# A chunked state scan feeding a gated two-layer product: the second scan moved ahead in the prologue, and the early loads gathered in one queue

## The chip, the cores and the metric

The kernel runs on one core of one Trainium2 chip. The metric is the device time of one execution in microseconds (us); lower is better. Five engines work side by side, each through its own list of instructions in order: TensorE (PE, matrix products), VectorE (DVE), ScalarE (ACT), GpSimd (POOL) and SyncE (SP, which here only issues loads and stores). An engine waits where an instruction needs something that another engine or a load has not finished yet. Loads and stores are moved by 16 DMA engines, and wait in the queue of the engine that issues them: SP's queue (with a few of ACT's) and POOL's.

## The reference

The first half is a state-space scan (Mamba-2's form) on x (4 batches, 8 heads, 768 steps, 32 wide), a decay a per head and step, and B and C (16 wide). Cut to what matters, per chunk:

```python
la = log(clip(a, 1e-6, 1)); cum = cumsum(la)
M = (C @ B.T) * exp(cum_i - cum_j) * causal       # inside a chunk
y = M @ x + (C @ state) * exp(cum)                # and from the chunks before
state = exp(sum(la)) * state + sum_j(B_j x_j * exp(cum_last - cum_j))
```

The result, 3072 tokens of 256 numbers, goes through two layers with float32 weights w_in (256 x 2048) and w_out (2048 x 256), which are given in double precision:

```python
h = x @ w_in
g = h * (1 / (1 + exp(-h)))                       # SiLU
out = g @ w_out
```

## The kernel before, in words

**Units and pairs.** The tokens are cut into 12 *units* of 256 (three to a batch). A unit's scan gives XF[u], its 256 tokens as input of the two layers. Units are taken in pairs: pair 0 is units 0 and 1. For pair 0 the two layers run in plain float32 products: f_s1(u, j) multiplies XF[u] with weight block j (j = 0 to 7, 256 columns of w_in) on PE and takes the SiLU on ACT; f_s2(j), "m" in the lists below, multiplies with weight block 8 + j of w_out. From pair 1 on, the products are split into three parts at a faster format (s1_h, s1_d, s2, s2_d), driven by step(s); that part of the kernel is not changed. There are two PSUM banks ("hp", function half) for the results of first products, so a product needs the bank whose SiLU, two products earlier, is done.

**A unit's scan.** Its steps are: f_TP or f_T (transposes of B and C, on PE or DVE, with copies on ACT), f_T2 (CE = C by head parity, ACT), f_Ek or f_E1 (E, the decay matrix, as a running scan on DVE), f_B (B times the last decay), f_P0 and f_P (clipping the decay, on POOL, and its running product pfx on DVE), f_C (C times pfx), f_G (C B^T, small products on PE into a bank "gy"), f_D0 (B^T x, the same bank), f_M (E times f_G's result, DVE, two halves), f_S (the state from chunk to chunk, DVE), f_SM (ACT), f_Y (all of it together on PE) and f_X (copy to XF on ACT). f_M and f_S need f_D0, and f_Y needs f_M, f_SM and f_C. E needs ab[u], the decay spread over partitions. For units 0 and 1 PE makes ab from ach (f_Ab); for unit 2 it is loaded back from a_first, a small copy of the first decays that f_A writes to DRAM; from unit 3 on from a_zero, which f_A3 writes together with a_in, the source of pz. So f_P of unit 3 and f_E1 of unit 3 need a round trip: load acl, clip it on POOL (f_A2), store a_in and a_zero (f_A3), and load pz (load_pa) and ab (load_ab) back.

**Weights.** A block n (0 to 15) is loaded in double precision (load_w, 512 KB, tile raw). ACT makes two parts of it (w_size: wu, wv), DVE three operations on them (w_bits), POOL the last addition, which gives the float32 block w32[n]. raw, and later the split inputs xh, xl, xd of a pair, share a ring of six buffers, so raw of block 6 takes the buffer of block 0, and so on: a load waits until its buffer's last reader is done.

**The order.** Nothing is scheduled automatically: each engine runs its instructions in the order in which this Python program names them. Lines 698 to 783 are the prologue: scan of unit 0, block 0 and so on, with the scan of unit 1 in between, written out by hand. Then `steps` (L844) names first products (u, j) with texts that say what is put behind each: "b5" is w_bits(5), "s6" w_size(6), "r10" the load of block 10, "2:T1" for unit 2 the stages T and 1, where a stage's letters are those of `stage` (T transposes, P pfx, 1 and 2 the halves of the scan E, B, C, D = f_G and f_D0, S, s = f_SM, M, Y = f_Y and f_X, h, l, d the split of XF, a = load_ab of the next unit, L all loads of a unit). A second list does the same for m0 to m5. busy(n) puts dummy products on PE.

Of the kernel before, what the change touches and what calls it, by code (L numbers as in the profile page):

```python
# [33 lines left out]
def kernel(  # L34
# [22 lines left out]
    nc = tc.nc  # L57
# [58 lines left out]
    def load_n(u, i, q, ks=(0, 1)):  # L116
        b, t0 = at(u)
        if i == 1:
            if u not in tbc:
                tbc[u] = block("tbc0")[:, 0:256].rearrange("p (k h n) -> p k h n", k=2, h=H)  # L120
        elif u not in bn:
            bn[u] = (block("bn0")[:, 0:256].rearrange("p (k h n) -> p k h n", k=2, h=H) if u in (0, 1, 3) else
                     loads.tile([128, 2, H, N], FP32, name="bn"))
        for k in ks:
            q.dma_start(out=(bn, tbc)[i][u][:, k], in_=(B, C)[i][b, :, t0 + 128 * k:t0 + 128 * k + 128].rearrange("h p n -> p h n"))
# [12 lines left out]
    def load_x(u, q, ks=(0, 1)):  # L138
        b, t0 = at(u)
        if u not in xt:  # L140
            xt[u] = loads.tile([128, 2, H, D], FP32, name="xt", bufs=2)
        for k in ks:
            q.dma_start(out=xt[u][:, k], in_=x[b, :, t0 + 128 * k:t0 + 128 * k + 128].rearrange("h p d -> p h d"))
# [31 lines left out]
    def load_w(n, q):  # L175
        j = n % 8
        src = wi[:, :, j * WF:(j + 1) * WF] if n < 8 else wo[:, 2 * j:2 * j + 2]
        if src.dtype == FP32:
            w32[n] = block("w32")
            q.dma_start(out=two(w32[n]), in_=src)  # L180
            return
        t = raw[n] = quad.tile([128, 2, WF, 2], U32, name="raw", tag="quad")
        q.dma_start(out=t.rearrange("p k f two -> p k (f two)"), in_=src.bitcast(U32))

    def w_size(n, what="uv"):
        if n in raw:
            if "u" in what:
                u = wu[n] = block("wu")
                nc.scalar.activation(two(u), raw[n][:, :, :, 1].bitcast(FP32), AF.Abs)
            if "v" in what:  # L190
                v = wv[n] = block("wv")
                nc.scalar.activation(two(v), raw[n][:, :, :, 0], AF.Copy, scale=2.0 ** -51, bias=2.0)

    def w_bits(n, parts=1):
        if n in raw:
            u, v, hi = two(wu.pop(n)), two(wv.pop(n)).bitcast(U32), raw[n][:, :, :, 1]
            w32[n] = block("w32")
            for i in range(parts):
                fs = slice(WF // parts * i, WF // parts * (i + 1))
                if i == 0 or n == 0:  # L200
                    ws = fs if n == 0 else slice(0, WF)
                    ui = u[:, :, ws].bitcast(U32)
                    nc.vector.tensor_scalar(out=u[:, :, ws], in0=u[:, :, ws], scalar1=LEAST, scalar2=MOST,
                                            op0=ALU.max, op1=ALU.min)
                    nc.vector.tensor_scalar(out=ui, in0=ui, scalar1=3, scalar2=None, op0=ALU.logical_shift_left)
                    nc.vector.scalar_tensor_tensor(out=v[:, :, ws], in0=hi[:, :, ws], scalar=0x80000000, in1=v[:, :, ws],  # L206
                                                   op0=ALU.bitwise_and, op1=ALU.bitwise_or)
                nc.gpsimd.tensor_tensor(out=two(w32[n])[:, :, fs].bitcast(U32), in0=u[:, :, fs].bitcast(U32),  # L208
                                        in1=v[:, :, fs], op=ALU.add)
# [42 lines left out]
    for n in range(2):  # L252
        load_w(n, nc.sync)
    load_a(1)
    load_w(2, nc.sync)
    load_w(3, nc.sync)
    load_x(1, nc.sync, (0,))

    def f_A():
        nc.vector.tensor_scalar(out=ach[A0:A1], in0=ach[A0:A1], scalar1=1.0, scalar2=1e-6, op0=ALU.min, op1=ALU.max)  # L260
        nc.vector.memset(ach[A0:A1, :, 0:1], 0.0)
        nc.sync.dma_start(out=a_first, in_=ach[A0:A1])
# [3 lines left out]
    def f_A1():  # L266
        for b in range(1, batch):
            nc.sync.dma_start(out=acl[NC0 * (b - 1):NC0 * b],
                              in_=bass.AP(tensor=a.tensor, offset=a.offset + b * H * S, ap=[[Q, NC0], [S, H], [1, Q]]))
# [51 lines left out]
    nc.scalar.activation(misc[:, 2 * UT - 1:], idle[:, 0:1], AF.Silu)  # L321
    early(6)
    f_A()
    hm = const.tile([128, H], FP32, name="hm")
    nc.gpsimd.memset(hm, 1.0)
    nc.gpsimd.affine_select(out=hm, in_=hm, pattern=[[-N, H]], compare_op=ALU.is_ge,
# [42 lines left out]
    def f_Ek(u, k, hs=slice(0, H)):  # L369
        scan_E(u, H * k + hs.start, hs.stop - hs.start, ab.pop((u, k, hs.start))[:, hs])  # L370
# [77 lines left out]
    def f_M(u, k):  # L448
        m = E[u].rearrange("p k (g e) t -> p k g (e t)", e=2)
        nc.vector.tensor_tensor(out=m[:, k], in0=DP[u][:, :, 128 * k:128 * k + 128], in1=m[:, k], op=ALU.mult)  # L450
# [78 lines left out]
    def f_s1(u, j):  # L529
        hp = two(half("hp"))  # L530
        for i in range(2):
            for kc in range(KC):
                nc.tensor.matmul(out=hp[:, i], lhsT=two(w32[j])[:, kc, 128 * i:128 * i + 128],  # L533
                                 rhs=two(XF[u])[:, kc], start=(kc == 0), stop=(kc == KC - 1))
        GT[u, j] = block("gT")
        nc.scalar.activation(two(GT[u, j]), hp, AF.Silu)
        if j == 7:
            XF.pop(u)
# [168 lines left out]
    for e in range(2):  # L707
        f_T2(0, e)
    nc.scalar.activation(BH[0], new_dp(0)[:, 2, 256:512], AF.Copy)
    load_w(4, nc.sync)  # L710
    load_ab(2, nc.sync)
    load_a(2)
    f_A1()
    f_Ek(0, 0, slice(4, 8))
    f_Ek(0, 1, slice(0, 4))
    busy(1, 10, acc("zero"))
# [7 lines left out]
    f_M(0, 0)  # L724
    w_size(0, "u")
    f_C(0, nc.gpsimd)
    load_x(1, nc.gpsimd, (1,))
    load_n(1, 1, nc.gpsimd)
    f_S(0)
    f_SM(0)  # L730
# [5 lines left out]
    f_Y(0)  # L736
    busy(2)
    f_X(0)
    load_n(2, 1, nc.gpsimd, (0,))
    f_Ek(1, 0)  # L740
    w_bits(1, 2)
    load_n(2, 1, nc.gpsimd, (1,))
    w_size(2)
    f_s1(0, 0)
    w_size(3)
    f_Ek(1, 1)
    w_bits(2, 2)
    f_s1(0, 1)
    f_TP(1)
    for e in range(2):  # L750
        f_T2(1, e)
    load_bcx(3, "c")
    for n in range(5, 8):
        load_w(n, nc.sync)
    f_B(1, nc.gpsimd)
    f_P0(1, nc.gpsimd)
    w_bits(3, 2)
    w_size(4)
    f_s1(0, 2)
    f_G(1)  # L760
    f_D0(1)
    w_bits(4, 2)
    f_P(1)
    f_C(1, nc.gpsimd)
    f_P0(2, nc.gpsimd)
    load_n(2, 0, nc.gpsimd)
    load_x(2, nc.gpsimd)
    f_A2(True)
    f_A2(False)
    f_A3()  # L770
    for n in range(8, 10):
        load_w(n, nc.sync)
    load_pa(3, nc.sync)
    f_S(1)
    f_SM(1)
    f_M(1, 0)
    f_M(1, 1)
    f_P(2)
    f_s1(0, 3)
    f_s1(0, 4)  # L780
    f_Y(1)
    f_X(1)
    w_size(5)

    def stage(u, what):
        for c in what:
            if c == "L":
                load_unit(u)
            elif c == "a":
                load_ab(u + 1, nc.sync)  # L790
            elif c == "n":
                load_n(u, 0, nc.gpsimd)
            elif c == "x":
                load_x(u, nc.gpsimd)
            elif c == "T":
                if 0 < u < UPB:
                    f_TP(u)
                else:
                    f_T(u, 0)
                    f_T(u, 1)  # L800
                f_T2(u, 0)
                f_T2(u, 1)
            elif c == "P":
                f_P(u)
            elif c in "12":
                f_E1(u, int(c) - 1, 2)
            elif c == "B":
                f_B(u)
            elif c == "C":
                f_C(u)  # L810
            elif c == "D":
                f_G(u)
                f_D0(u)
            elif c == "M":
                f_M(u, 0)
                f_M(u, 1)
            elif c == "S":
                f_S(u)
            elif c == "s":
                f_SM(u)  # L820
            elif c == "Y":
                f_Y(u)
                f_X(u)
            elif c == "h":
                f_xh(u)
            elif c == "l":
                f_xl(u)
            elif c == "d":
                f_xd(u)
# [4 lines left out]
    def todo(text):  # L834

        for step in text.split():
            if ":" in step:
# [3 lines left out]
            n = int(step[1:].split(".")[0])  # L841
            {"b": w_bits, "s": w_size, "h": w_h, "l": w_l, "d": w_d, "v": partial(w_d, vector=True), "m": f_s2, "p": s1_d, "r": load_r}[step[0]](n)

    steps = ((1, 0, "2:T1 b5 s6"), (1, 1, "2:C2Ba r10"), (1, 2, "3:nx b6 r11 s7"), (1, 3, "2:DSsM r12"),  # L844
             (1, 4, "b7 r13 s8"), (0, 5, "3:T s9"), (1, 5, "2:Y b8 r14"), (0, 6, "3:1PC s10"),
             (1, 6, "b9 r15 3:2B s11 h0 l0"), (0, 7, "2:h s12"), (1, 7, "3:D b10 3:SsM"))
    for u, j, text in steps:
        f_s1(u, j)
        todo(text)
    for text in ("m0 b11 s13 2:l h1 l1", "m1 3:Y b12 s14 2:d d0 4:L 3:h h2 l2", "m2 b13 s15 3:l d1 h3 l3",  # L850
                 "m3 b14 3:d d2 h8 l8 v3", "m4 b15 p0 d8 h4 l4 v4 h5 l5", "m5 4:T v5 h9 l9 v9"):
        todo(text)

# [113 lines left out]
```

## Time and profile before

| | before |
|---|---|
| median of 3 runs | 336.48 us (336.42 to 336.59) |
| the profiled execution | 336.49 us, its span 334.8 us |
| PE busy | 322.5 us (96%) |
| DVE, ACT, POOL busy | 251.8 us (75%), 220.9 us (66%), 92.0 us (27%) |
| loads and stores | 31.87 MB, mean 95 GB/s |

Of the 1.7 us between span and time nothing is shown in the profile. The profile's page gives the busy share of each engine in 40 equal slices of the span, the clock that PE was granted, the costliest groups of instructions with what ended the idle time before them, and the chain of work that ended last, followed back from the end. Shares of the whole span say little about a change at the start: its stretch of the timeline has to be read by itself. The costliest groups belong to pairs 1 to 5. The prologue with all of pair 0, up to the first split product (L561), takes the first 77.6 us.

### The profile page before, as it was taken

The page shows a single profiled execution, that of the slowest core. Times are in us where ns is not written, and L with a number is a line of the kernel's source. Part 1 is how long each engine was busy: PE and PEld are TensorE (multiplying, and loading weights), DVE is VectorE, ACT ScalarE, POOL GpSimd, SP SyncE. Part 2 cuts the span into 40 slices and gives each one's busy share as a digit, 9 for nine tenths or more (in the row PEclk, how much of TensorE's full clock was granted, in tenths as well). Part 3 has the DMA queues.
Part 4 walks back from the last instruction along what each step waited for, and adds up shares of the span by engine and source line. Part 5 has one row for each costly group of instructions (what it writes and reads, how often), then busy time and mean ns, then how long its engine had stood idle before and what let it go on. Part 6 is the DMA issues. An engine that isn't in the chain of part 4 may idle for free.

```text
span 334.8 us, 7981 instructions
## 1 busy us (share of the span) xinstructions
PE 322.5 (96%) x3219; PEld 261.0 (78%) x3221; DVE 251.8 (75%) x413; ACT 220.9 (66%) x422; POOL 92.0 (27%) x96
## 2 busy tenths in 40 slices
PE   8787799999999999999999999999999999999996
PEld 4455688888878778778788778788878788899995
DVE  7997379987787888997965996965996873484443
ACT  3665377596578898756676766667666756656662
POOL 6789625467211222231202231202230202000000
PEclk9999799999999999999999999999999999999999
DMA  6956994867884585163430164420263000012001
GB/s 142 287 168 204 268 290 154 165 115 127 166 159 81 102 157 91 47 112 70 102 54 0 47 112 85 104 38 0 53 107 65 2 2 0 0 25 40 0 2 63
DMA packets 79700, 31.87 MB, mean 95 GB/s; under 512 B 63168, under 2 KB 70080, under 8 KB 79664
## 3 DMA queue, kind: packets, MB, share of 16 engines
q1 hardware_dynamic: 73856, 24.42, 31.6%
q0 software_dynamic: 3440, 6.56, 10.5%
q10 hardware_dynamic: 2368, 0.39, 0.6%
q8 instruction: 25, 0.41, 0.5%
q14 instruction: 11, 0.09, 0.1%
HBM read 22.79 MB, written 3.32 MB: 78 GB/s over the span
## 4 chain that ended last, share of the span: by engine, by line
PE 90%; DVE 3%; POOL 3%; DMA 2%; issue 1%; POOLq 0%; DVEq 0%
PE hp L569 23%; PE hp L561 11%; PE oa L610 9%; PE oa L611 9%; PE b L641 9%; PE oa L546 8%; PE hp L533 6%; PE gy L493 2%; PE b L636 2%; DMA bn<-in_B_dram 2%; PE b L619 2%; PE oa L619 2%; PE gy L444 2%; POOL w L208 2%; PE gy L484 2%; PE gy L430 1%
## 5 line engine op out<-in xcount | busy, mean ns | idle before, releaser
L563 ACT ACTIVATE hp<-hp 128x512 f32<-128x512 f32 x80 | 46.6, 582 | 70.1 <-PE hp L561 70.1
L583 DVE TENSOR_TENSOR gl<-g,gh 128x512 fp32r<-128x512 f32 x62 | 42.8, 690 | 50.3 <-ACT gh L579 47.3
L569 PE MATMUL hp<-xh,wh 128*128 128x512 f32 x160 | 65.4, 409 | 0.0
L587 DVE SCALAR_TENSOR_TENSOR gd<-gh,g 128x512 fp32r<-128x512 f32 x80 | 59.5, 747 | 5.1 <-ACT gh L579 5.1
L583 POOL TENSOR_TENSOR gl<-g,gh 128x512 fp32r<-128x512 f32 x18 | 29.4, 1632 | 121.4 <-ACT gh L579 121.4
L569 PE MATMUL hp<-xl,wl 128*128 128x512 f32 x160 | 62.7, 392 | 0.0
L579 ACT ACTIVATE gh<-g 128x512 fp32r<-128x512 f32 x80 | 50.6, 632 | 2.7
L610 PE MATMUL oa<-gh,wh 128*128 128x512 f32 x128 | 50.0, 390 | 0.0
L611 PE MATMUL oa<-gl,wl 128*128 128x512 f32 x128 | 49.9, 390 | 0.0
L561 PE MATMUL hp<-xd,wd 128*128 128x512 f32 x160 | 49.6, 391 | 0.0
L577 ACT ACTIVATE g<-hp 128x512 f32<-128x512 f32 x80 | 47.5, 594 | 0.6 <-PE hp L569 0.6
L569 PEld LDWEIGHTS hp<-xh,wh 128*128 128x128 f32 x160 | 30.0, 188 | 8.8 <-ACT hp L563 2.6
L561 PEld LDWEIGHTS hp<-xd,wd 128*128 128x128 f32 x160 | 30.0, 188 | 6.6
L533 PE MATMUL hp<-xf,w 128*128 128x256 f32 x128 | 31.3, 397 | 3.7 <-POOL w L208 2.8
L641 PE MATMUL b<-gd,wd 128*128 128x512 f32 x128 | 34.5, 389 | 0.0
L569 PEld LDWEIGHTS hp<-xl,wl 128*128 128x128 f32 x160 | 30.1, 188 | 4.8
L533 PEld LDWEIGHTS hp<-xf,w 128*128 128x128 f32 x128 | 24.4, 197 | 9.2 <-POOL w L208 5.2
L358 DVE TENSOR_TENSOR_SCAN E<-ab,diag 128x512 f32<-128x512 f32 (+1 forms) x26 | 29.2, 1153 | 2.4 <-PE gy L493 1.6
L208 POOL TENSOR_TENSOR w<-wu,wv 128x512 uint32<-128x512 uint32 (+1 forms) x21 | 24.3, 1165 | 21.0 <-DVE wv L206 18.4
L546 PE MATMUL oa<-gT,w 128*128 128x256 f32 x128 | 28.8, 381 | 0.0
L610 PEld LDWEIGHTS oa<-gh,wh 128*128 128x128 f32 x128 | 24.0, 188 | 5.1
L611 PEld LDWEIGHTS oa<-gl,wl 128*128 128x128 f32 x128 | 24.0, 188 | 5.1
(104 smaller groups left out, 474.1 us busy)
## 6 DMA issues: line engine op xcount, KB each, us to landing
ab<-a_zero SPq DMA_DIRECT2D x18, 256.0 KB
raw<-in_moe_w_in_dram SPq DMA_DIRECT2D x8, 512.0 KB
raw<-in_moe_w_out_dram SPq DMA_DIRECT2D x8, 512.0 KB
wl<-w POOLq DMA_DIRECT2D x16, 256.0 KB, 4.0
out_dram<-ot SPq DMA_DIRECT2D x40, 64.0 KB
xt<-in_x_dram SPq DMA_DIRECT2D x19, 128.0 KB
tbc<-in_C_dram SPq DMA_DIRECT2D x40, 32.0 KB
pz<-a_in SPq DMA_DIRECT2D x9, 130.0 KB
```

Source lines behind the costliest of these rows:

```text
L533: nc.tensor.matmul(out=hp[:, i], lhsT=two(w32[j])[:, kc, 128 * i:128 * i + 128], rhs=two(XF[u])[:, kc], start=(kc == 0), stop=(kc == KC - 1))
L546: nc.tensor.matmul(out=OA[0][m][:, UT * u:UT * u + UT], lhsT=two(w32[8 + j])[:, i, 128 * m:128 * m + 128], rhs=two(GT[u, j])[:, i], start= ...
L561: nc.tensor.matmul(out=HP[s], lhsT=two(WD[f // 2])[:, kc, 128 * (f % 2):128 * (f % 2) + 128], rhs=XD[P][:, kc], start=(kc == 0), stop=Fals ...
L563: nc.scalar.activation(HP[s], HP[s], AF.Copy, scale=HALF / UP)
L569: nc.tensor.matmul(out=HP[s], lhsT=two(w[f // 2])[:, kc, 128 * (f % 2):128 * (f % 2) + 128], rhs=x_[P][:, kc], start=False, stop=(kc == KC ...
L577: nc.scalar.activation(G[s], HP.pop(s), AF.Silu, scale=UP)
L579: nc.scalar.activation(GH[s], G[s], AF.Copy, scale=DOWN)
L583: engine.tensor_tensor(out=GL[s], in0=G[s], in1=GH[s].bitcast(FP32), op=ALU.subtract)
L587: nc.vector.scalar_tensor_tensor(out=GD[s], in0=GH[s].bitcast(FP32), scalar=1.0 + 1.0 / HALF, in1=G.pop(s), op0=ALU.mult, op1=ALU.subtract)
L610: nc.tensor.matmul(out=OA[P][m], lhsT=two(WH[n])[:, r, ms], rhs=gh, start=(f == 0), stop=False)
L611: nc.tensor.matmul(out=OA[P][m], lhsT=two(WL[n])[:, r, ms], rhs=gl, start=False, stop=(f == NF - 1))
L641: nc.tensor.matmul(out=B2[P][:, m], lhsT=two(WD[n])[:, r, 128 * m:128 * m + 128], rhs=gd, start=(fresh and s == tiles[0]), stop=True, skip ...
```

## The change

- The scan of unit 1 (f_TP, f_T2, both halves of E, and all up to f_X(1)) stands between blocks 1 and 2 instead of being spread over blocks 1 to 4. Only f_s1(0, 0) and f_s1(0, 1) stand before it; four dummy products (busy(4)) stand before f_Y(1).
- Behind it the products of the two units take turns by block: (1,0), (1,1), (0,2), (1,2), (0,3), (1,3) and so on; before, unit 0's products 0 to 4 came first. The stages of units 2 and 3 and the weight steps are spread anew over this list, and the scan of unit 3 is finished (f_Y(3)) before m0 instead of behind m1.
- The loads of x of unit 1 (half of it), and of B, C and x of units 2 and 3, go from POOL's queue to SP's. SP's queue is put in a new order: a_first, x of unit 1, block 2, ab, pa and acl for later units, block 3, C, B and x of unit 2, block 4, C and B of unit 3 for the transposes (load_bcx(3, "c")), block 5, the copies of f_A3, pz and B of unit 3, block 6, x of unit 3, ab of unit 3, block 7 and the rest. POOL's queue keeps B and C of unit 1.
- f_P0(1), f_P0(2) and f_A2 move with the scan of unit 1.

The number of instructions on DVE and ACT is the same; PE has four dummy products more.

```diff
--- before.py
+++ after.py
@@ -252,9 +252,6 @@
     for n in range(2):
         load_w(n, nc.sync)
     load_a(1)
-    load_w(2, nc.sync)
-    load_w(3, nc.sync)
-    load_x(1, nc.sync, (0,))
 
     def f_A():
         nc.vector.tensor_scalar(out=ach[A0:A1], in0=ach[A0:A1], scalar1=1.0, scalar2=1e-6, op0=ALU.min, op1=ALU.max)
@@ -321,6 +318,7 @@
     nc.scalar.activation(misc[:, 2 * UT - 1:], idle[:, 0:1], AF.Silu)
     early(6)
     f_A()
+    load_x(1, nc.sync)
     hm = const.tile([128, H], FP32, name="hm")
     nc.gpsimd.memset(hm, 1.0)
     nc.gpsimd.affine_select(out=hm, in_=hm, pattern=[[-N, H]], compare_op=ALU.is_ge,
@@ -707,10 +705,13 @@
     for e in range(2):
         f_T2(0, e)
     nc.scalar.activation(BH[0], new_dp(0)[:, 2, 256:512], AF.Copy)
-    load_w(4, nc.sync)
+    load_w(2, nc.sync)
     load_ab(2, nc.sync)
     load_a(2)
     f_A1()
+    load_w(3, nc.sync)
+    load_n(2, 1, nc.sync)
+    load_n(2, 0, nc.sync)
     f_Ek(0, 0, slice(4, 8))
     f_Ek(0, 1, slice(0, 4))
     busy(1, 10, acc("zero"))
@@ -724,7 +725,6 @@
     f_M(0, 0)
     w_size(0, "u")
     f_C(0, nc.gpsimd)
-    load_x(1, nc.gpsimd, (1,))
     load_n(1, 1, nc.gpsimd)
     f_S(0)
     f_SM(0)
@@ -736,51 +736,41 @@
     f_Y(0)
     busy(2)
     f_X(0)
-    load_n(2, 1, nc.gpsimd, (0,))
-    f_Ek(1, 0)
+    load_x(2, nc.sync)
+    load_w(4, nc.sync)
+    load_bcx(3, "c")
+    load_w(5, nc.sync)
+    f_P0(1, nc.gpsimd)
     w_bits(1, 2)
-    load_n(2, 1, nc.gpsimd, (1,))
-    w_size(2)
     f_s1(0, 0)
-    w_size(3)
-    f_Ek(1, 1)
-    w_bits(2, 2)
-    f_s1(0, 1)
     f_TP(1)
     for e in range(2):
         f_T2(1, e)
-    load_bcx(3, "c")
-    for n in range(5, 8):
-        load_w(n, nc.sync)
+    f_Ek(1, 0)
+    f_Ek(1, 1)
+    f_s1(0, 1)
     f_B(1, nc.gpsimd)
-    f_P0(1, nc.gpsimd)
-    w_bits(3, 2)
-    w_size(4)
-    f_s1(0, 2)
     f_G(1)
     f_D0(1)
-    w_bits(4, 2)
     f_P(1)
     f_C(1, nc.gpsimd)
     f_P0(2, nc.gpsimd)
-    load_n(2, 0, nc.gpsimd)
-    load_x(2, nc.gpsimd)
     f_A2(True)
     f_A2(False)
-    f_A3()
-    for n in range(8, 10):
-        load_w(n, nc.sync)
-    load_pa(3, nc.sync)
+    f_M(1, 0)
     f_S(1)
     f_SM(1)
-    f_M(1, 0)
     f_M(1, 1)
-    f_P(2)
-    f_s1(0, 3)
-    f_s1(0, 4)
+    w_size(2)
+    busy(4)
     f_Y(1)
     f_X(1)
-    w_size(5)
+    w_bits(2)
+    f_A3()
+    load_pa(3, nc.sync)
+    load_n(3, 0, nc.sync)
+    load_w(6, nc.sync)
+    load_x(3, nc.sync)
 
     def stage(u, what):
         for c in what:
@@ -788,10 +778,6 @@
                 load_unit(u)
             elif c == "a":
                 load_ab(u + 1, nc.sync)
-            elif c == "n":
-                load_n(u, 0, nc.gpsimd)
-            elif c == "x":
-                load_x(u, nc.gpsimd)
             elif c == "T":
                 if 0 < u < UPB:
                     f_TP(u)
@@ -841,13 +827,13 @@
             n = int(step[1:].split(".")[0])
             {"b": w_bits, "s": w_size, "h": w_h, "l": w_l, "d": w_d, "v": partial(w_d, vector=True), "m": f_s2, "p": s1_d, "r": load_r}[step[0]](n)
 
-    steps = ((1, 0, "2:T1 b5 s6"), (1, 1, "2:C2Ba r10"), (1, 2, "3:nx b6 r11 s7"), (1, 3, "2:DSsM r12"),
-             (1, 4, "b7 r13 s8"), (0, 5, "3:T s9"), (1, 5, "2:Y b8 r14"), (0, 6, "3:1PC s10"),
-             (1, 6, "b9 r15 3:2B s11 h0 l0"), (0, 7, "2:h s12"), (1, 7, "3:D b10 3:SsM"))
+    steps = ((1, 0, "2:P1 s3"), (1, 1, "b3 s4 2:T2"), (0, 2, "2:BCa r7 b4 s5"), (1, 2, "2:DSsM r8 r9"),
+             (0, 3, "b5 s6 r10"), (1, 3, "2:Y 3:T r11"), (0, 4, "3:P1 b6 s7 r12"), (1, 4, "3:C2B"), (0, 5, "b7 r13 s8"),
+             (1, 5, "3:DSsM 2:h"), (0, 6, "b8 r14 s9 h0 l0"), (1, 6, "3:Y"), (0, 7, "b9 r15 s10 s11"), (1, 7, "b10 s12"))
     for u, j, text in steps:
         f_s1(u, j)
         todo(text)
-    for text in ("m0 b11 s13 2:l h1 l1", "m1 3:Y b12 s14 2:d d0 4:L 3:h h2 l2", "m2 b13 s15 3:l d1 h3 l3",
+    for text in ("m0 b11 s13 2:l h1 l1", "m1 b12 s14 2:d d0 4:L 3:h h2 l2", "m2 b13 s15 3:l d1 h3 l3",
                  "m3 b14 3:d d2 h8 l8 v3", "m4 b15 p0 d8 h4 l4 v4 h5 l5", "m5 4:T v5 h9 l9 v9"):
         todo(text)
```

## The prediction

> **What bounds the kernel now.** I read the page first, then the chain of work that ended last, PE's waits and timeline up to 90 us, the windows around PE's longest wait, the queues of SP and POOL, and last the landing time of each early load (the trace's semaphore updates, load by load).
>
> From the page, the busy tenths of PE, the granted clock and the DMA share in 40 slices of 8.4 us, and the chain by engine:
>
> ```profile
> PE   8787799999999999999999999999999999999996
> PEclk9999799999999999999999999999999999999999
> DMA  6956994867884585163430164420263000012001
> PE 90%; DVE 3%; POOL 3%; DMA 2%; issue 1%; POOLq 0%; DVEq 0%
> ```
>
> PE is the bound. It has holes only in the first five slices; after 36 us it waits for nothing until the end. So the change can win only what PE idles before 36 us, and loses whatever it makes PE idle later. PE's waits up to 90 us (total, times, longest):
>
> ```profile
> PE gy L396 <- DMA bn<-in_B_dram: 3.6, 1, 3.6
> PE hp L533 <- POOL w L208: 2.8, 3, 1.7
> PE hp L533 <- ACT xf L503: 0.8, 2, 0.5
> ```
>
> The 3.6 us are unit 2's transposes (L396). Their B load is issued from POOL at 27.74 us, behind all POOL did before, and lands at 35.5:
>
> ```profile
> 27.74 7.73 DMA bn<-in_B_dram
> 35.61 1.19 PE gy L396 x4
> 36.81 6.30 PE hp L533 x24
> ...
> 44.08 5.38 PE hp L533 x24
> ```
>
> The same 24 records take 6.30 us after that wait and 5.38 us later. The windows say why (PE busy first, clock before the DMA share): one window of 3.42 us held no matmul, and the next ran at half clock.
>
> ```profile
> 32.11:35.53 3.42, 0.00 (x0) 0.00 (x0) 1.22 (x2) 0.51 (x1) 2.89 (x4) 1.00 1.01 276
> 35.53:38.94 3.41, 3.33 (x10) 2.77 (x11) 0.95 (x2) 2.10 (x5) 2.63 (x4) 0.50 1.05 347
> ```
>
> So the hole costs 3.6 us and half of 3.3 us, some 5.3 us. Last, how slowly the small copies of f_A3 and what waits for them pass SP's queue:
>
> ```profile
> 28.01 0.44 SPq L283 DMA_DIRECT2D a_in<-misc  x1
> 32.06 0.31 SPq L284 DMA_DIRECT2D a_in<-acl  x1
> 32.98 0.30 SPq L285 DMA_DIRECT2D a_zero<-acz  x1
> 33.37 0.91 SPq L183 DMA_DIRECT2D raw<-in_moe_w_out_dram  x2
> 37.35 0.62 SPq L106 DMA_DIRECT2D pz<-a_in  x1
> 39.57 1.26 SPq L113 DMA_DIRECT2D ab<-a_zero  x2
> ```
>
> pz is issued when a_in<-acl has landed (37.3), 5.2 us after that copy's issue; ab<-a_zero, issued at 39.6 and 40.2, lands at 45.2 and 46.4. Before, unit 3's first scan wants it only at 50.9.
>
> **The base.** The profiled execution took 336.49 us, 1.7 over its span of 334.8; the median is 336.48. I compare one point of equal work: all 16 first products, the scans' Y of units 1 to 3, and the start of m0, f_s2(0). Before, m0 starts at 58.98 with Y(3) (0.51 + 0.79 us) still to come: 60.3. From there the instructions are the same, and PE waits for nothing in the trace.
>
> **Early part: what it wins.** f_s1(0,0) keeps its place (13.5 to 15.3). f_TP(1) now stands before f_s1(0,1) and needs unit 1's C. That load moves up 0.9 us in POOL's queue, since half of x of unit 1 leaves it; it landed at 17.9, so 17.0 (17.9 if traffic sets its latency, 15.5 at the earliest, when the B load ahead of it landed). So PE waits 1.7 us here. w_bits(1) now runs before the two scans of unit 1 (1.14 us each), so block 1 is ready by 16.4 and the old 1.66 us wait for it goes. f_s1(0,1) runs 17.2 to 19.0, ACT's copies (1.6 us, as at 19.70 to 21.30) lie beside it, f_G and f_D0 (0.62 + 0.40) end at 20.2. Next PE needs M, S and SM of unit 1. For unit 0, D0's end to Y's start was 2.7 us (8.52 to 11.23); POOL's work beside pfx and st made them 1.22 and 1.23 us where 0.69 and 0.92 are usual, so 2.7 to 3.5, and I take 3.4. Before, products covered this chain; now only busy(4), 0.9 us of dummies, lies in it, so they cost nothing. Y(1) runs 23.6 to 25.0 and, after X (0.5), f_s1(1,0) starts at 25.5.
>
> What is left then: 14 products at 1.79 us (7.17 for four), transposes 0.44, two f_G + f_D0 at 1.02, Y(2) 1.41, Y(3) 1.30: 30.2 us, so m0 at 55.7 instead of 60.3. **4.6 us won** if nothing waits after 25.5. Blocks 2 to 5 seem safe: a block now feeds two products (3.6 us), and a block's ACT, DVE and POOL steps take 1.15 + 1.5 + 1.3.
>
> **The one queue: what it gives back.** B, C and x of units 2 and 3 and half of x of unit 1 move from POOL's queue to SP's. In the built program each SP load also waits for the load eight places ahead of it (eight semaphores in turn). The f_A3 copies, pz of unit 3 and ab of unit 3 now stand behind all of that. Prices, from landings behind one another: a weight block 1.3 us (47.41 to 48.68) to 2.9 (15.15 to 18.04, POOL's loads beside); half an x 0.7 to 1.4; half a B or C 0.6 to 0.9; half an ab 1.0 to 1.45; a pa 0.75; acl 0.6. From raw1's landing at 11.8: pa1 and x1 2.4, raw2 2.2, ab2 2.5, pa2 and acl 1.3, raw3 1.5, B and C of unit 2 3.2, x2 1.8, raw4 1.5: 28.2. The quiet prices are too low under load: from 11.8 to 18.25 the old queue moved some 4.2 us of HW loads, with POOL's 1.5 or so beside. I take 29.2 for raw4.
>
> The eighth C/B load of unit 3 waits for raw4, raw5 stands behind it (issue 29.7), then the copies (30 to 31), landing 3.7 us later behind raw5 (2.5 to 3.0 alone, 4.6 to 5.2 before): 34.5. Only then come pz3, B of unit 3, raw6, x3, ab3 and raw7 (issues 34.5 to 38.5). Data: pz3 36.8, B 38.2, raw6 39.7 (last part 40.5), x3 41.3, ab3 44. An ab issue stood 1.62 us (usually 0.6) behind two B loads at 61.73, so I put ab3 at **45.0** and raw7 at 46.5.
>
> Who wants these: ACT's queue has w_size(6) between the Silus of (0,3) and (1,3), wanted at 36.6 and held to 40.5; w_size(7) between (0,4) and (1,4), wanted about 41.5. There are two hp banks, so a held Silu holds the second next product. DVE wants ab3 at 39.5 and stands until 45.0; behind it lie, in order, scan 1.22, w_bits(6) 1.5, cw 0.42, scan 1.22, BT 0.42, w_bits(7) 1.5, S 1.15, M 1.28, w_bits(8) 1.5: 10.2, and 10.7 with three overlapping adds of POOL. End 55.7. xh of unit 2 takes raw8's buffer and waits for that; behind it on ACT are xh 0.53, Silu(0,6) 0.5, w_size(9) 1.15, wh and wl 1.04, Silu(1,6) 0.5, then f_s1(1,7), 1.79: m0 at 61.2, against 60.3. The 4.6 us are given back, and 0.9 more. **336.49 + 0.9 = 337.4.** Neither the removed hole nor its half clock returns: they are inside the 60.3.
>
> The Trainium skill, "DMA: Bandwidth & Descriptors", section "Anatomy of one DMA", prices the moving of data at bytes over 436e9 a second, 0.15 us for half a B and 0.3 for half an x; by it, as an estimate, six halves of B and C (0.65 us less each) and six of x (0.5 less) would bring ab3 some 6.9 us sooner and the change to about 332. Its section "Specifications" speaks against that and against this change: transfers need 512 bytes for line rate, and these runs are of 64 and 128 bytes. The rows, 0.6 and 0.7 at least, side with the second.
>
> **Bounds of the queue.** At the lowest of these prices throughout, raw4 is there at 25.0 and, with the copies back in 3 us, ab3 at 38.5: nothing is held, m0 is at 55.7, 331.9 us. At prices a quarter above mine up to raw4, it lands at 32.3 (11.8 + 20.5), ab3 at 48.1, m0 at 64.3: 340.5. Above 39.5 m0 moves one for one with ab3, as DVE is full behind it. I stay near the middle, a little late, since last parts of a load lagged its first by 1.3 to 4.2 us whenever the queue stayed full (raw3: 13.86 to 18.04).
>
> **Rivals.** (1) *The queue keeps pace; faster.* No POOL load is beside SP's after 17 us, and the worst prices above all come from times with both. If ab3 lands before 43.4, the change wins: m0 is 16.2 us behind ab3, so 41 to 43 give 333.4 to 335.4, about 334.5. For: 1.3 us per block in the quiet stretch from 46 us. Against: SP's queue needs 73856 packets for 24.42 MB and POOL's 3440 for 6.56 MB (the page's queues), so the moved loads cost more packets than before, and the copies' round trip (3 to 5 us) stays. Chance 0.31. (2) *A draw*, ab3 between 43.4 and 44.8: 336.5; 0.13. (3) *My case*, ab3 44.8 to 47: 337.4, up to 339.3; 0.43. (4) *The queue is late and a PE wait fills a whole clock window*: w_size(6) or (7) held beyond 4 us, half clock again, 1.7 us more: 340.5; 0.13. For it: the pattern of 32 to 39 us. Against: products of two units keep PE's waits short, at 2 us or so each. That the change does not do what it says is excluded by the built order: the products alternate as described.
>
> **How the numbers follow.** 0.2%, 0.7 us, is about what a measurement of this kernel can tell from no change. Faster by more is rival 1, 0.31; within, rival 2, 0.13; slower, 0.43 + 0.13 = 0.56. The range leaves out the tail of rival 1 below 333.6 and of rival 4 above 340.8. My case alone: 337.2 to 339.3.
>
> **What would show it.** (Lines of the changed kernel.) Right: no wait of L394 (f_TP of unit 2) for bn; f_s1(1,0) near 25.5 with 2 to 2.5 us of PE idle before Y(1); no half clock near 36; then waits of PE for ACT between 40 and 60 us, ACT's L189 idle on raw near 40 and 46, DVE's L356 idle on ab until about 45, m0 at 61.2. Wrong: ab3 landed by 42 (rival 1), PE idle 1.7 us or more beyond that in one piece with a window at 0.50 (rival 4), f_s1(1,0) after 27 (the early chain is mis-sized), or PE waiting after m0, which I put at nothing.

## The result and the profile after

The changed kernel took 340.31 us (median of 4 runs, 339.6 to 342.22) against 336.45 us of the kernel before on the same chip: ratio 1.0125, 95% interval [1.0083, 1.0167] (as recorded; the quotient of the two medians is 1.0115). Slower, as forecast, and inside the range, but by 3.9 us where the likeliest case said 0.9. The profiled execution is the longest of the four: 342.22 us, 1.9 over the median, its span 340.3.

The page of the profile after: PE's busy tenths and the granted clock in 40 slices of 8.5 us, and the chain by engine.

```profile
PE   8879849999999999999999999999999999999996
PEclk9999986999999999999999999999999999999999
PE 82%; DMA 8%; SPq 3%; DVE 3%; ACT 2%; issue 1%; DVEq 0%
```

The hole that stood in the fourth and fifth slice is gone, and a larger one stands in the sixth (42.5 to 51 us), with the lowered clock behind it. PE's share of the chain fell from 90% to 82%; DMA and SP's queue took most of what it lost. PE's waits up to 100 us (total, times, longest):

```profile
PE hp L531 <- ACT gT L534: 6.8, 5, 3.5
PE gy L482 <- DVE E L448: 1.8, 1, 1.8
PE gy L394 <- DMA tbc<-in_C_dram: 0.9, 2, 0.6
```

L394 waits for bn no more. The new bound is L531, a first product waiting until L534, the SiLU of the product two places earlier, has cleared its bank. In ACT's timeline (start, length, in brackets the idle time before and who ended it) the reason stands directly ahead of that SiLU:

```profile
41.65 0.66 ACT L189 ACTIVATE wu<-raw 128x512 f32<-128x512 f32 x1 [4.64 <-DMA raw<-in_moe_w_in_dram]
...
49.02 0.67 ACT L189 ACTIVATE wu<-raw 128x512 f32<-128x512 f32 x1 [3.84 <-DMA raw<-in_moe_w_in_dram]
...
50.14 1.06 ACT L534 ACTIVATE gT<-hp 128x512 f32<-128x512 f32 x2
```

These are w_size(6) and w_size(7), each held by its block's load, raw6 and raw7. PE's timeline shows the product (1,5) released behind the second, and what the clock does to it and to f_G of unit 3 (L442, 0.70 us for unit 2):

```profile
50.77 3.78 PE L531 MATMUL hp<-xf,w 128*128 128x256 f32 x8 [3.48 <-ACT gT L534]
54.48 1.16 PE L442 MATMUL gy<-ce,bh 32*64 32x128 f32 x32
```

Eight records of L531 take 3.78 us where eight took 1.99 elsewhere. The windows around it (PE's busy time first, then PEld, DVE, ACT and POOL; clock, DMA share and GB/s at the end):

```profile
45.92:49.33 3.41, 1.37 (x7) 0.86 (x5) 3.02 (x6) 0.32 (x1) 0.37 (x1) 1.00 1.01 359
49.33:52.74 3.41, 1.97 (x5) 1.61 (x6) 3.34 (x5) 2.98 (x6) 1.02 (x1) 0.50 1.03 395
52.74:56.16 3.42, 3.42 (x69) 2.10 (x67) 0.55 (x1) 0.60 (x1) 1.26 (x1) 0.50 0.66 231
```

Two windows at half clock, after one in which PE was still busy for 40%. Last, why the two blocks are late: SP's queue from f_A3's copies on, one line for each issue.

```profile
31.49 0.36 SPq L281 DMA_DIRECT2D a_in<-acl  x1
...
35.53 0.63 SPq L106 DMA_DIRECT2D pz<-a_in  x1
...
37.40 1.01 SPq L183 DMA_DIRECT2D raw<-in_moe_w_in_dram  x1
...
39.64 2.49 SPq L113 DMA_DIRECT2D ab<-a_zero  x2
42.23 0.54 SPq L183 DMA_DIRECT2D raw<-in_moe_w_in_dram  x1
```

After the last of the copies nothing is issued for 3.2 us, until a_in<-acl is back (35.5). raw6, ab and raw7 follow, and land at 41.6, 46.2 and 49.0. m0 starts at 65.80 us, after Y(3): 5.5 us behind the 60.3 of the kernel before. What follows takes 342.22 - 65.80 = 276.4 us, against 276.2 before: in this execution everything was lost ahead of m0.

### The profile page after: what moved, and what is told of

The parts are those of the page before. It is cut to its first block, busy times and chain, and to the rows that moved or that the text cites. A ratio compares the mean times of both kernels' runs of the same rounds, so it can differ in the third digit from the quotient of the medians.

```text
span 340.3 us, 7984 instructions
## 1 busy us (share of the span) xinstructions
PE 325.5 (96%) x3222; PEld 261.6 (77%) x3225; DVE 250.0 (73%) x413; ACT 220.2 (65%) x422; POOL 81.8 (24%) x82
## 4 chain that ended last, share of the span: by engine, by line
PE 82%; DMA 8%; SPq 3%; DVE 3%; ACT 2%; issue 1%; DVEq 0%
PE hp L567 23%; PE hp L559 11%; PE oa L608 9%; PE oa L609 9%; PE b L639 9%; PE oa L544 8%; DMA raw<-in_moe_w_in_dram 3%; DMA ab<-a_first 2%; PE b L634 2%; PE b L617 2%; PE oa L617 2%; PE gy L491 2%; PE gy L442 2%; PE hp L531 2%; DMA a_first<-ach 2%; PE gy L482 1%
## 5 line engine op out<-in xcount | busy, mean ns | idle before, releaser
L581 DVE TENSOR_TENSOR gl<-g,gh 128x512 fp32r<-128x512 f32 x62 | 42.7, 689 | 50.3 <-ACT gh L577 47.3
L585 DVE SCALAR_TENSOR_TENSOR gd<-gh,g 128x512 fp32r<-128x512 f32 x80 | 59.5, 747 | 5.2 <-ACT gh L577 5.2
L581 POOL TENSOR_TENSOR gl<-g,gh 128x512 fp32r<-128x512 f32 x18 | 29.2, 1621 | 122.2 <-ACT gh L577 122.2
L575 ACT ACTIVATE g<-hp 128x512 f32<-128x512 f32 x80 | 47.4, 593 | 0.6 <-PE hp L567 0.6
L531 PE MATMUL hp<-xf,w 128*128 128x256 f32 x128 | 32.7, 405 | 7.3 <-ACT gT L534 6.8
L356 DVE TENSOR_TENSOR_SCAN E<-ab,diag 128x512 f32<-128x512 f32 (+1 forms) x26 | 30.5, 1205 | 7.4 <-DMA ab<-a_zero 6.6
L531 PEld LDWEIGHTS hp<-xf,w 128*128 128x128 f32 x128 | 24.3, 198 | 13.6 <-ACT gT L534 8.2
L208 POOL TENSOR_TENSOR w<-wu,wv 128x512 uint32<-128x512 uint32 (+1 forms) x18 | 24.9, 1384 | 32.5 <-DVE wv L206 32.5
L639 PEld LDWEIGHTS b<-gd,wd 128*128 128x128 f32 x128 | 24.0, 188 | 5.1
```

What stands on the lines that cost most here:

```text
L575: nc.scalar.activation(G[s], HP.pop(s), AF.Silu, scale=UP)
L581: engine.tensor_tensor(out=GL[s], in0=G[s], in1=GH[s].bitcast(FP32), op=ALU.subtract)
L585: nc.vector.scalar_tensor_tensor(out=GD[s], in0=GH[s].bitcast(FP32), scalar=1.0 + 1.0 / HALF, in1=G.pop(s), op0=ALU.mult, op1=ALU.subtract)
L639: nc.tensor.matmul(out=B2[P][:, m], lhsT=two(WD[n])[:, r, 128 * m:128 * m + 128], rhs=gd, start=(fresh and s == tiles[0]), stop=True, skip ...
```

## The experiments

Each run is compared with the kernel before on the same chip (its median is 336.45 us in the first comparison, 336.8 to 337.3 in the others). Ratios are over 4 to 11 executions of each version, and differ a little from the quotients of medians; m0, landings and half clock are of the one profiled execution, which lies up to 2.2 us from its run's median. m0 is the start of f_s2(0) in the profiled execution (for the kernel before and its variant with the end of Y(3)); landings are the trace's last semaphore update of a load.

| run | ratio to the kernel before, 95% interval | m0 | ab of unit 3 | raw7 | half clock ahead of m0 |
|---|---|---|---|---|---|
| the change, first comparison | 1.0125 [1.0083, 1.0167] | 65.8 | 46.2 | 49.0 | 49.3-56.2 |
| the change again (e8) | 1.0058 [1.0037, 1.0078] | 63.5 | 47.0 | 48.6 | 24.9-31.7 |
| e11, dummies alone | 1.0079 [1.0050, 1.0108] | 64.3 | 45.4 | 48.4 | 51.1-54.5 |
| e4, dummies in the wait | 1.0066 [1.0029, 1.0103] | 65.1 | 46.3 | 47.5 | 21.9-28.7, 45.7-49.2 |
| e5, w_size later | 1.0057 [1.0030, 1.0083] | 63.9 | 46.3 | 47.4 | 24.0-30.8, 51.3-58.1 |
| e6, unit 3's B and x in POOL | 0.9996 [0.9970, 1.0023] | 60.7 | 44.1 | 46.3 | 23.9-30.7 |
| e3, copies early | 0.9986 [0.9966, 1.0007] | 59.6 | 41.8 | 45.2 | 23.8-30.7 |
| e7, e3 + e6 + dummies | 0.9974 [0.9952, 0.9996] | 58.5 | 42.0 | 43.0 | none |
| e2, the kernel before, unit 2 in SP | 0.9954 [0.9921, 0.9986] | 59.5 | 50.3 | 39.4 | 38.0-41.4 |
| e1, units 2 and 3 in POOL | 0.9941 [0.9918, 0.9963] | 58.2 | 41.8 | 42.8 | none |
| e10, e7 + ACT's tail | 0.9924 [0.9892, 0.9955] | 59.3 | 44.6 | 45.6 | none |
| e9, e1 + dummies + ACT's tail | 0.9907 [0.9878, 0.9937] | 57.5 | 39.6 | 40.6 | none |

**e1: the loads back to POOL, the new order kept.**

```diff
-    load_n(2, 1, nc.sync)          # behind block 3
-    load_n(2, 0, nc.sync)
...
     f_C(1, nc.gpsimd)
+    load_n(2, 1, nc.gpsimd)
+    load_n(2, 0, nc.gpsimd)
     f_P0(2, nc.gpsimd)
     f_A2(True)
     f_A2(False)
+    load_x(2, nc.gpsimd)           # and no load_x(2, nc.sync)
...
-    load_n(3, 0, nc.sync)
+    load_n(3, 0, nc.gpsimd)
-    load_x(3, nc.sync)
+    load_x(3, nc.gpsimd)
```

> The changed kernel with one part undone: B, C and x of unit 2 and B and x of unit 3 are issued from POOL again, behind the steps of unit 1's scan there; the order of the products and the scan's place stay. Theory (the one queue costs the gain): block 4's raw lands 4 to 6 us earlier than 29.7, ab of unit 3 near 38 to 40 instead of 46.2, raw7 near 42; ACT is not held at w_size(7), no window at half clock near 49 to 56, m0 near 56 to 58, and the time is 332 to 334. Rival (the new order itself holds PE: w_size(6) and w_size(7) stand ahead of Silus, and the splits wait for DVE): m0 stays above 61 and the time is 338 or more. Second rival (POOL is late with unit 2's B, as before the change): PE stands at unit 2's transposes for 2 us or more and the time is 335 to 337.

Ratio 0.9941: the loss turns into a gain. f_A3's copies are issued at 27.3 instead of 31.0, ab lands at 41.8, later than the 38 to 40 expected, and raw7 at 42.8. Two of PE's waits up to 100 us:

```profile
PE gy L442 <- DVE cw L412: 1.5, 1, 1.5
PE hp L531 <- ACT gT L534: 1.4, 2, 0.8
```

The 6.8 us for ACT are 1.4. m0 at 58.2 is inside the 56 to 58 expected but for 0.2; 335.55 us is 1.8 under the kernel before on that chip, less than the 332 to 334 expected. PE now waits 1.5 us for unit 2's cw (f_C), which is part of it, and the profiled execution, 334.58 us, is the shortest of its six. With the order of products kept, the loss is gone: the queue, not that order, costs the change its gain.

**e2: the kernel before, with unit 2's loads alone moved to SP.**

```diff
     load_a(2)
     f_A1()
+    load_n(2, 1, nc.sync)
+    load_n(2, 0, nc.sync)
...
     f_X(0)
+    load_x(2, nc.sync)             # the four POOL calls for unit 2 removed
     f_Ek(1, 0)
```

> The kernel before with one part of the change alone: B, C and x of unit 2 are issued from SP behind block 4, as early as the SP queue allows; the order of products and scans is that of before. Theory (the hole of 3.6 us and its half clock were the queue's fault and can be had back without the new order): no wait of PE for bn, no half clock at 35.5, m0 3 to 5 us earlier, 331.5 to 333.5. Rival (every load of small runs put into SP's queue delays the blocks behind it by what it wins): blocks 5 to 7 land 3 us later, PE waits for them instead, 336 to 338.

Between the two: 0.9954. PE no longer waits for bn, but for ACT, 3.1 us instead of 3.6, by its waits up to 100 us:

```profile
PE hp L533 <- ACT gT L536: 3.1, 1, 3.1
```

The clock falls behind it as it did before, from 38.0 to 41.4, after a window with 1.18 us of PE. ACT waits there for raw5, which landed at 35.1 where it had landed at 30.4. The small loads in SP's queue moved the hole from one load to another, as the rival said; the 1.5 us that the time fell by were not in either's numbers.

**e3: SP's queue in another order, f_A3's copies earlier, nothing else.**

```diff
-    load_bcx(3, "c")               # both from behind block 4
-    load_w(5, nc.sync)
...
     f_A2(True)
     f_A2(False)
+    f_A3()
+    load_w(5, nc.sync)
+    load_bcx(3, "c")
...
-    f_A3()
     load_pa(3, nc.sync)
-    load_n(3, 0, nc.sync)
     load_w(6, nc.sync)
-    load_x(3, nc.sync)
+    load_n(3, 0, nc.sync)
...
-    (1, 1, "b3 s4 2:T2"), (0, 2, "2:BCa r7 b4 s5")
+    (1, 1, "b3 s4 2:T2ax r7"), (0, 2, "2:BC b4 s5")   # x: load_x of the next unit
```

> The changed kernel with SP's queue in another order and nothing else: the copies of f_A3 stand directly behind f_A2, ahead of block 5 and of unit 3's C for the transposes; pz of unit 3, block 6 and B of unit 3 follow, and x and ab of unit 3 stand ahead of block 7. Theory (the late copies hold ab of unit 3, and DVE behind ab holds the rest): ab lands at 37 to 40 instead of 46.2, DVE stands less than 1 us for it, m0 near 57 to 59, 333 to 335.5. Rival (the queue's whole work is what is late, block 7 above all, since ACT's w_size(7) stands ahead of a Silu): ab comes earlier but raw7 still lands at 47 to 49, PE waits 3 us and its clock drops, 338.5 to 341.

0.9986, at the kernel before's time. ab came at 41.8 (37 to 40 expected: pz was issued 2.5 us after the copies were back, behind unit 3's eight C and B loads), DVE no longer stood for it, raw7 came at 45.2, and PE's wait for ACT fell to 1.3 us. m0 is 6.2 us ahead of the first profile's and 5.5 ahead of e4's, from the order of SP's queue alone: the three small copies earlier, ab and block 7 one step earlier, x of unit 3 behind ab. Which of these moves wins how much is not told apart. And this execution still lost 3 us to half clock: the products (1,0) and (1,1) took 6.76 us instead of 3.72. The windows, of PE alone:

```profile
20.42:23.84 3.42, 1.59 (x98) 1.00 0.83 141
23.84:27.25 3.41, 2.94 (x22) 0.50 0.85 120
```

The 1.83 us wait for M of unit 1 sits in the first of them. In the changed kernel's first profile that wait fell across a window's edge and cost no clock.

**e4: dummies in the place of the 3.48 us wait.**

```diff
     for u, j, text in steps:
+        if (u, j) == (1, 5):
+            busy(14, 0, acc("zero"))
         f_s1(u, j)
```

> The changed kernel with 14 dummy products on PE (about 3 us) in the place where it stood 3.48 us for ACT, ahead of the product (1,5); nothing else is changed. Theory (the two windows at half clock from 49.3 to 56.2 are worth about 2.6 us of the profiled 342.2, 1.8 in one product and 0.5 in a small one among them): no window at half clock there, m0 2 to 2.7 us earlier, 337.5 to 338.5. Rival (the clock is no part of it, since DVE and ACT end later than PE in that stretch and xh of unit 2 waits for DVE until 60.2 anyway): the clock is full and the time stays within 0.7 us of 340.3, or is 1 us longer by the dummies.

Inconclusive on its own question. In the profiled execution the clock fell earlier (45.7 to 49.2), (1,4) and (0,5) took 5.41 us, and no hole was left for the dummies: they ran from 49.8 to 52.6, on PE's path. m0 is 0.7 us sooner than in the first profile, 1.6 later than in e8. The granted clocks of its ten executions say more: four, at 0.985 to 0.988, took 341.2 to 342.6 us, six, at 0.989 to 1.000, took 337.9 to 339.3. So a low clock goes with a long execution there, whichever causes the other; but the two at 0.999 and 1.000 took 338.3 and 339.3, still 1.0 and 1.9 us over the kernel before.

**e5: ACT's order alone.**

```diff
-    (0, 3, "b5 s6 r10"), (1, 3, "2:Y 3:T r11"), (0, 4, "3:P1 b6 s7 r12"), (1, 4, "3:C2B"), (0, 5, "b7 r13 s8")
+    (0, 3, "b5 r10"), (1, 3, "s6 2:Y 3:T r11"), (0, 4, "3:P1 b6 r12"), (1, 4, "3:C2B"), (0, 5, "s7 b7 r13 s8")
```

> The changed kernel with ACT's order alone changed: w_size(6) stands behind the Silu of (1,3) and w_size(7) behind that of (0,5), each one or two Silus later, so that no Silu of these stands behind a block that has not landed; the loads are as in the changed kernel. Theory (the late ab and raw7 set the end by way of DVE: ab at 46, raw7 near 48, then the scans and w_bits; PE's held products and its half clock add about 3 us to it, as they make f_D0 of unit 3 late): PE no longer stands for ACT at 43 and 50, f_D0 of unit 3 comes 2 to 4 us sooner, xh of unit 2 is released 2 to 3 us sooner, and the time is 2 to 3 us under the changed kernel's. Rival A (the order on ACT is the whole cause): m0 near 58, 5 us or more under the changed kernel. Rival B (the lateness of the loads alone decides): PE's wait only moves to f_D0 of unit 3 or to (0,6), m0 and the time stay within 1 us of the changed kernel's.

Rival B: 1.0057, the same as e8 beside it (1.0058). PE no longer stands for ACT; by its timeline it stands for BT of unit 3 (what f_B makes), behind the scans that want ab:

```profile
52.04 0.68 PE L428 MATMUL gy<-xt,BT 64*32 64x64 f32 x32 [2.89 <-DVE BT L380]
```

f_D0 of unit 3 starts at 52.0, against 53.0 in e8. Two chains end at it: raw7, w_size(7), SiLU, (1,5), and ab, two scans, BT. The reordering of the first leaves the second.

**e6: unit 3's B and x alone in POOL's queue.**

```diff
-    load_n(3, 0, nc.sync)
+    load_n(3, 0, nc.gpsimd)
-    load_x(3, nc.sync)
+    load_x(3, nc.gpsimd)
```

> The changed kernel with B and x of unit 3 alone issued from POOL; unit 2's B, C and x stay with SP. In the changed kernel these four loads landed at 39.2 to 42.8, between pz and ab of unit 3. Theory (the four loads stand in the way of ab and raw7 with their moving time of 2 to 3 us): ab lands near 43.5, raw7 near 46, m0 2 to 4 us earlier, 336 to 338.5. Rival (the copies of f_A3, which land at 35.5, set ab by themselves, and B and x cost nothing): ab at 45 or later, m0 and the time within 1 us of the changed kernel's.

As the theory said, 44.1 for ab and 46.3 for raw7, 2.9 and 2.3 us ahead of e8 on the same chip, though pz was issued 0.2 us later; 336.82 against 338.95 us. Counted from pz's issue, ab lands after 7.3 us here, and after 10.2 to 11.2 in the five executions that have all four loads in SP's queue. PE waits 1.2 us for ACT instead of 3.6. The Trainium skill, "DMA: Bandwidth & Descriptors", section "Anatomy of one DMA", written for the GpSimd path, prices moving data at bytes over 436e9 a second; by that alone these four loads would take some 0.9 us (an estimate: 0.15 for half a B, 0.3 for half an x). The run shows 2.3 to 2.9.

**e7: early copies, unit 3's B and x in POOL, 11 dummies.** The edits of e3 and e6 (x of unit 3 now from POOL, behind f_A3), and:

```diff
-    busy(4)
+    busy(11)
     f_Y(1)
```

> Three edits of the changed kernel together: f_A3's copies directly behind f_A2, B and x of unit 3 from POOL, and 11 instead of 4 dummy products before f_Y(1), so that the clock window with the 1.83 us wait for M of unit 1 keeps enough work. Theory (the early copies and the shorter queue bring ab of unit 3 to 39 to 40.5 and raw7 to 42 to 43, and no window falls to half clock): m0 near 56 to 57, 2 to 3.5 us less than the kernel before on the same chip, and no run with a window at half clock in the prologue. Rival (POOL's loads collide with SP's between 27 and 34 us, as those of both queues did before 17 us): ab at 41.5 or later, m0 at 58 or later, no better than the variant with unit 2's loads in POOL too, 2 us under the kernel before.

0.9974, between theory and rival: raw7 at 43.0 as expected, ab at 42.0 and m0 at 58.5 as the rival had it. The dummies do what they should: by PE's timeline the wait for M is 0.32 us, and the window over it, from 19.14 us, holds 3.10 us of PE at full clock.

```profile
21.99 0.69 PE L482 MATMUL gy<-cw,sm 32*64 32x64 f32 x32 [0.32 <-DVE E L448]
```

**e8: the changed kernel again.**

> The changed kernel itself once more, for a comparison on the same chip. Theory (a late raw7 and a hole of PE at 46 to 50 that drops the clock in most executions): 1.0 to 1.3% over the kernel before, two windows at half clock in most runs, ab of unit 3 at 45 to 46.5, raw7 at 47 to 49. Rival (the profiled 342.2 was an odd run, and raw7's late last part with it): within 0.5% of the kernel before, raw7 at 46.5.

1.0058: slower again, but by half as much as in the first comparison; the expectation was too high and its rival too low. ab and raw7 land late again (47.0, 48.6). Here the clock fell early instead, from 24.9 on, and not behind the late wait. The window ahead of the fall holds the last 0.5 us of the wait for M of unit 1 and a pause of 1.56 us in the middle of f_Y(1), for which the profile names no cause. The windows of PE, and then PE's timeline at f_Y(1) and at (1,5):

```profile
21.45:24.87 3.42, 1.35 (x95) 1.00 0.45 83
24.87:28.28 3.41, 2.94 (x34) 0.50 0.71 86
```

```profile
24.59 0.69 PE L491 MATMUL gy<-E,xt 64*32 64x64 f32 x35 [1.56 <-issue]
...
50.41 1.99 PE L531 MATMUL hp<-xf,w 128*128 128x256 f32 x8 [1.66 <-ACT gT L534]
```

The early 3 us cost little at (1,5): they come out of the later wait, 1.66 instead of 3.48 us, since (1,5) starts when raw7 allows it.

**e9 and e10: the last waits before m0.** In e1 and e7, PE still waited 0.77 and 0.59, or 0.91 and 0.60 us, for SiLUs behind xh of unit 2, which itself waits 2.2 us for w_bits(8). Both got the same edit, e9 the 11 dummies too:

```diff
-    (1, 5, "3:DSsM 2:h"), (0, 6, "b8 r14 s9 h0 l0"), (1, 6, "3:Y")
+    (1, 5, "3:DSsM"), (0, 6, "b8 2:h r14"), (1, 6, "s9 h0 l0 3:Y")
```

> The variant with the loads of units 2 and 3 in POOL's queue, with two further edits: 11 instead of 4 dummy products before f_Y(1), and xh of unit 2 and the steps w_size(9), wh, wl each one Silu later on ACT, so that the Silu of (0,6) no longer stands behind the 2.2 us that xh waits for w_bits(8). Theory (PE's last two waits for ACT before m0, 0.77 and 0.59 us, and their drains come from that order): both go, m0 near 56.5 instead of 58.2, the ratio to the kernel before near 0.990. Rival (what xh, w_size(9), wh and wl take from ACT only moves behind the Silu of (1,6), and blocks 9 and 10 come later to m1 and m2): PE waits 1 us or more in m1 or m2, ratio 0.994 or more, as without these edits.

> The variant with early copies, unit 3's B and x from POOL and 11 dummies, with the same edit on ACT: xh of unit 2 and w_size(9), wh and wl one Silu later. Theory: PE's waits of 0.9 and 0.6 us before m0 go, m0 near 57 instead of 58.5, the ratio to the kernel before near 0.993 (0.9974 without it). Rival: as for the other variant, the wait moves to m1 or m2, ratio 0.997 or more.

0.9907 and 0.9924, as the theory said, though e9's interval overlaps that of e1 and e10's that of e7. From (0,6) on, PE's timeline of e9 shows no wait:

```profile
48.99 3.72 PE L531 MATMUL hp<-xf,w 128*128 128x256 f32 x16
...
53.93 3.72 PE L531 MATMUL hp<-xf,w 128*128 128x256 f32 x16
57.49 17.43 PE L544 MATMUL oa<-gT,w 128*128 128x256 f32 x80
```

m0 is at 57.5 (56.5 expected). In e10's profiled execution it was at 59.3, not near 57: ab came 2.6 us later than in e7, so its ratio rests on all eleven executions (median 335.0 us). They fall into two groups, five at 332.4 to 333.2 us and six at 335.0 to 336.6, at much the same clock (0.998 to 1.000, 0.995 to 1.000); why is open. e9 has the lowest ratio of all versions that were run: 333.75 us, 3.1 under the kernel before on that chip.

**e11: the changed kernel with 11 dummies.** The edit of busy alone.

> The changed kernel with 11 instead of 4 dummy products before f_Y(1), and nothing else. Theory (the 1.83 us hole there drops the clock for two windows where the windows fall so that one holds under 1.65 us of PE's work, in some executions only; but the late loads set the end, so PE gets that time back as longer waits for ACT): no window at half clock between 20 and 32 us, yet the time stays within 1 us of the changed kernel's, ratio to before 1.004 to 1.009. Rival (the early drop is what the changed kernel loses): 1.5 us or more under the changed kernel, ratio 1.001 or less.

As the theory said: no half clock before 51 us, and 1.0079. PE waited for ACT later on, as before:

```profile
50.19 2.97 PE L531 MATMUL hp<-xf,w 128*128 128x256 f32 x8 [3.23 <-ACT gT L534]
```

raw7 landed at 48.4, and 48.4 + 1.75 is this line's start. Work or clock won ahead of a late load is returned as waiting for it. Two of the six executions were granted the full clock (1.000), and took 339.48 and 340.38 us: with no whole window at half clock the changed order still loses 2.6 us and more to the kernel before (336.87 on that chip).

## Why the prediction was right, and what it mis-sized

**Right.** The early part: no wait for bn, no half clock at 36 us, the wait before Y(1) 1.83 us (2 to 2.5 said) and f_s1(1,0) at 24.8 (25.5 said; 23.9 to 26.1 over the runs with this order), though PE's wait for C of unit 1 was 0.9 us and not 1.7. That the queue gives it back: raw4 at 29.7 (29.2), the copies home at 35.5 (34.5), raw6 at 41.6 (40.5 for its last part), ab at 46.2 (45.0; 45.4 to 47.0 in the five executions with this SP order). That nothing waits behind m0: 276.4 us against 276.2, in the profiled execution. And e1, e3 and e6 show the cause by changing the loads' queue or their order alone.

**Mis-sized: raw7 and what hangs on it.** The sum went by ab and DVE, ab + 16.2, with "raw7 at 46.5" beside it. The chain of raw7 was named (w_size(7), two hp banks) but never summed, and in the profiled execution it is the one that was last. By the profile it runs so: raw7's landing, 1.75 us for w_size(7) and one SiLU, (1,5); from there some 13.0 us to m0 where no window was at half clock (an estimate from e8, 63.45 - 50.41, in which PE still stood 1.3 us for SiLUs behind xh). From 46.5 that gives 46.5 + 1.75 + 13.0 = 61.3, the predicted m0 (61.2) by another road. Measured: raw7 at 49.0, 2.5 later; (1,5) at 50.77; 15.0 to m0, 2.0 more, with two windows at half clock. 2.5 + 2.0 is the 4.6 that m0 was off by, but for 0.1. This divides up the longest of the four executions, and not the ratio.

Of the 2.5, ab's lateness is 1.2. The other 1.3 is the price of the block behind ab: raw7's first part landed at 46.4, its last at 49.0, 2.8 us after ab, where 1.5 had been taken, near the quiet price. The bounds given were 1.3 to 2.9, and in the other four executions it was 1.2, 1.2, 1.6 and 3.1. The DMA engines were as full in all five (share 0.97 to 1.05 from 45 to 52 us), so that does not tell the high price from the low one; what does is open.

**"DVE is full behind it" held in two executions of five.** In e8 and e5 DVE did not stand between ab and w_bits(8), and xh of unit 2 started 10.8 us behind ab's landing, as the sum had it (10.7). In e8 m0 came 5.65 us after that (5.5 said): its miss of 2.3 us is ab's lateness, 2.0, and little else. In the first profile, e11 and e4 DVE stood 2.2 to 3.1 us for f_D0 of unit 3, which PE ran late, and xh started 13.1 to 14.0 us behind ab. ACT's timeline at xh, in e8 and in the first profile:

```profile
57.80 0.63 ACT L514 ACTIVATE xh<-xf 128x512 fp32r<-128x512 f32 x1 [2.21 <-DVE wv L206]
60.16 0.63 ACT L514 ACTIVATE xh<-xf 128x512 fp32r<-128x512 f32 x1 [2.21 <-DVE wv L206]
```

The two chains are nearly equal, and which is last changes with the execution: the number was right for a reason that was half of it.

**Rival 4 was priced too low.** The 340.31 us lie inside the range by 0.5, but outside "my case alone" (337.2 to 339.3), which had the chance of 0.43; they are rival 4's 340.5. That the range caught them is owed to the room left for this rival. e8's ratio, by contrast, would be 338.4 here (an estimate, 1.0058 x 336.45), my case. Rival 4 had 0.13 and asked for a wait beyond 4 us that fills a window; a hole of 3.48 us that left 40% of a window busy did it, at some 2.0 us (1.7 said). "Products of two units keep PE's waits short, at 2 us or so each" was true of the first wait (2.07), not of the second.

**Open.** In the first comparison the change's ratio was 1.0125, in e8 1.0058, and the intervals do not meet. One profile of each shows the clock falling in different places, but not why four executions of the first agree on the larger loss. The mean granted clock does not tell them apart: 0.989 to 0.990 in these four, 0.983 to 0.995 in e8's eight.

## What to carry to other kernels

Moving loads into one queue "by need" pays, as these runs show it, only if every load behind them has slack: a round trip through memory (store, wait, load back) belongs as early in the queue as its data exists, and small loads of short runs belong in another queue if that has room. When a load is late, sum every chain that starts at it, the one through a shared bank on the bound engine as well as the one through data, for removing one shows the next. Time won ahead of such a wait, by clock or by work, is not won.

## What the hardware showed that was not expected

**A window need not be empty to lower the clock.** Windows were 3.413 us long wherever a trace shows a whole one at half clock, and their edges fell at 3.5 to 6.8 us of the span (modulo the window) from execution to execution. In the 13 profiles there are some 1200 pairs of windows next to each other, up to 326 us. At full clock, the eleven windows with PE busy for 1.59 us or less (0.00, 0.87, and 1.18 to 1.59) were each followed by one at half clock, and none of those with 1.69 (then 1.75 twice, 1.76, 1.95) or more: the edge is just under half of a window. At half clock, the seven windows in which PE was busy for 1.97 to 2.94 us were followed by another at half clock, the eleven with 3.33 or more by full clock; halved, that is the same edge, though this reading is an inference. The Trainium skill, "TensorE: Matmul & The Clock Gate", Part 1, gives the same length and says that the windows run freely, which the traces bear out. It has the clock fall after an idle window, and its section "Why this matters for your kernels" advises against gaps above about 3 us. Here the one wait of 1.83 us before Y(1) did it in four of the seven profiles of the changed kernel and its variants with four dummy products, where the windows' edges let one window hold all or nearly all of the wait; in a fifth, e8, it took the pause of 1.56 us as well. Seven more dummies, 1.5 us of products that nobody wanted, kept all four profiles that had them from it.

**Where many loads are in flight, a block's parts spread.** raw7's 16 parts landed over 2.6, 0.5, 1.0, 1.0 and 2.4 us in five executions of the same queue order, and the waiting engine needs the last: in the first profile it landed at 48.99, and w_size(7) began at 49.02.
